# Four heads interleaved per group of cells, with K and V transposed four heads at a time, in an attention backward kernel

## Chip, cores and metric

One core of one Trainium2 chip. The metric is the time of one execution on the device, in microseconds (us); lower is better.

## The reference

Two independent blocks A and B of multi-head attention, each over 8 batches (b) of 96 queries with 32 heads (h) of 128 dimensions and a cache of 512 keys and values; forward output and all gradients, in bf16.

```python
def ref(x, k_cache, v_cache, wq, wo):        # x 8x96x640, caches 8x32x512x128
    q = (x @ wq).reshape(B, Sq, H, Dh).transpose(0, 2, 1, 3)
    p = softmax(einsum("bhqd,bhkd->bhqk", q, k_cache) * Dh ** -0.5)
    o = einsum("bhqk,bhkd->bhqd", p, v_cache)
    return o.transpose(0, 2, 1, 3).reshape(B, Sq, H * Dh) @ wo
# result: concat of blocks A and B, and its vjp with grad_out:
# dx, dk_cache, dv_cache, dwq, dwo of both blocks
```

Of the traffic, K and V are read twice each (once transposed), and dK and dV are written once: 256 KB per pair of heads and batch for each of them.

## The kernel before: what the change and the argument touch

The work is cut into 512 cells, one for each block, head and batch. A cell passes through stages in successive ticks. Two heads interleave, so 16 ticks carry two heads over 8 batches. The head work (projections, transposes of weights, gradients of the weights) is laid between the cells by a table of ticks.

```python
OFF = dict(t=-1, kn=3, vn=0, s2=3, s3=3, s4=4, s5=5, s6=6, s7=7, s8=8)   # tick offsets
HP = 2                                     # heads that interleave
TB = 2                                     # batches whose transposes are issued together

def p_ldT(h, b, which):                    # transposing DMA, K or V of HP heads
    t_ = kvp.tile([128, F4 * KC, 16], BF16, name=key + "_p", bufs=(4 if which == 0 else 6))
    src = (kc if which == 0 else vc)[b, h:h + HP].rearrange("h (r f) d -> (h r) (f d)", r=R8)
    nc.sync.dma_start_transpose(t_[:], src)                 # R8 = 16 // HP

def p_ldn(h, b, which):                    # plain load of the same K or V
    t_ = kvp.tile([128, HP, KC, 128], BF16, name=key, bufs=4)
    nc.sync.dma_start(...)

def p_st(h, b, which):                     # store of dV (1) or dK (0) of two heads
    nc.sync.dma_start(dst.rearrange("h (p c) d -> p h (c d)", c=KC), t_[:])

def c_s7(h, b):                            # dK, then evacuated by ACT
    ...
    st["dK_p"] = wk.tile([128, HP, KC * 128], BF16, name="dK_sb", bufs=2)
    nc.scalar.activation(dK_p[:, j], dK_ps[:], ACT.Identity, scale=1.0)
```

Note that every DMA above is issued by SP, one after the other: transposes, plain loads and stores (of the 1538 issues on SP in the trace of this kernel, no two overlap). dK_sb has two buffers, each for two heads.

## Time and profile before

| | |
|---|---|
| time, median of 2 runs | 1772.82 us (1771.46 to 1774.17) |
| span of the profiled run | 1763.2 us |
| PE content (instruction counts times their undisturbed durations) | 1591 us |
| transposing DMAs | 512 of 256 KB, 16 packets of 16 KB each |
| time for which SP is held by one of them | 1.75 us in the mean, 896 us in all |

The page and the waits are shown in the prediction below. What matters later and is not there is SP's own timeline. This is a stretch of it from the trace of the kernel before, with ACT's two evacuations of dK for one pair of heads (columns: start, duration, engine, line, operation, and in brackets the idle time before it):

```profile
641.02 0.60 ACT L428 ACTIVATE dK_sb<-dK_ps 128x512 bf16<-128x512 f32 x1
645.14 0.59 ACT L428 ACTIVATE dK_sb<-dK_ps 128x512 bf16<-128x512 f32 x1
```

```profile
645.22 3.01 SPq L246 DMA_TRANSPOSE KT_p<-in_A_k_cache_dram  x1
648.33 0.54 SPq L257 DMA_DIRECT2D V_sb<-in_A_v_cache_dram  x1
648.95 0.42 SPq L266 DMA_DIRECT2D out_dram<-dK_sb  x1
```

The pair of dK is complete at 645.73 us. Its store is issued at 648.95, 3.2 us later, after a transpose of K that held SP for 3.01 us and a plain load. What stands behind the transpose in SP's queue isn't issued in that time. Here the store still landed before ACT needed its buffer.

### The profile page before, as it was taken

Reading aid. Unit: us, or ns where it says so; the run is one execution under the profiler, and the core shown is the slowest. Engines: PE = TensorE matmul, PEld = TensorE weight load, DVE = VectorE, ACT = ScalarE, POOL = GpSimd, SP = SyncE. Lnnn points to the kernel's source line nnn. Section 1 sums busy time; section 2 is a strip of 40 time slices with the busy share of each in tenths; the row PEclk is TensorE's granted clock in tenths of the full one; section 3 lists DMA queues with packets and bytes.
Section 4 is the critical chain, followed back from the end, with each engine's and each line's share of the span. In section 5 each row is a group of like instructions: output and inputs, shape, how many; then the busy total and the mean of one; then the engine's idle time right before and its main releaser. Section 6 shows DMA issues by size and latency. Waiting matters only on the chain. (4 is left out here: it accounts for less than half of the span.)

```text
span 1763.2 us, 59487 instructions
## 1 busy us (share of the span) xinstructions
PE 1643.4 (93%) x22474; PEld 1371.8 (78%) x22648; DVE 1392.3 (79%) x3597; ACT 1349.2 (77%) x3529; POOL 712.9 (40%) x1306
## 2 busy tenths in 40 slices
PE   5899989999999999998998999999999989999997
PEld 4787878788888888786886787877878878787776
DVE  4786868878888888887886778787888878888885
ACT  4888967878778787875876898786787867878782
POOL 3343434433433443434365344343443334343336
PEclk9899999999999999999999999999999999999999
DMA  9999999999999999999999999999999999999983
GB/s 267 262 280 258 265 251 262 270 261 273 266 266 284 264 268 257 273 271 259 242 278 282 262 268 273 249 268 252 264 265 269 262 239 265 267 269 246 263 249 111
DMA packets 320609, 458.39 MB, mean 260 GB/s; under 512 B 37216, under 2 KB 300896, under 8 KB 312128
## 3 DMA queue, kind: packets, MB, share of 16 engines
q1 hardware_dynamic: 304672, 404.75, 87.7%
q0 software_dynamic: 15648, 49.83, 8.4%
q8 instruction: 177, 2.90, 0.7%
q14 instruction: 112, 0.92, 0.1%
HBM read 161.09 MB, written 159.12 MB: 182 GB/s over the span
## 5 line engine op out<-in xcount | busy, mean ns | idle before, releaser
L298 ACT ACTIVATE E_sb<-S_ps,negm 96x512 bf16<-96x512 f32 x512 | 349.2, 682 | 212.6 <-DVE negm L288 203.6
L317 POOL TENSOR_SCALAR P_sb<-E_sb,rinv 96x512 bf16<-96x512 bf16 x512 | 354.2, 692 | 343.8 <-DVE rinv L308 339.4
L371 POOL TENSOR_TENSOR prod<-OT_h,dOT_h 128x96 bf16<-128x96 bf16 x512 | 188.1, 367 | 571.6 <-DVE OT_h L343 563.0
L385 DVE SCALAR_TENSOR_TENSOR dS_sb<-dP_ps,dl_ps,P_sb 96x512 bf16<-96x512 f32 x512 | 382.1, 746 | 35.4 <-PE dl_ps L383 22.4
L288 DVE TENSOR_REDUCE negm<-S_ps 96x1 f32<-96x512 f32 x512 | 347.9, 680 | 67.4 <-PE S_ps L286 66.6
L428 ACT ACTIVATE dK_sb<-dK_ps 128x512 bf16<-128x512 f32 x512 | 302.6, 591 | 108.9 <-PE dK_ps L423 70.4
L362 ACT ACTIVATE dV_sb<-dV_ps 128x512 bf16<-128x512 f32 x512 | 307.8, 601 | 26.0 <-DMA out_dram<-dV_sb 23.3
L346 ACT ACTIVATE PT_sb<-optp_ps 128x384 bf16<-128x384 bf16 x512 | 252.1, 492 | 0.9 <-PE optp_ps L340 0.5
L286 PE MATMUL S_ps<-KT_p,QT_h 128*96 128x512 bf16 x512 | 197.1, 385 | 18.6 <-ACT dK_sb L428 18.1
L357 PE MATMUL dV_ps<-dOnat_h,P_sb 96*128 96x128 bf16 x2048 | 200.4, 221 | 6.1 <-ACT dV_sb L362 6.1
L423 PE MATMUL dK_ps<-Qnat_h,dS_sb 96*128 96x128 bf16 x2048 | 199.9, 221 | 6.1 <-ACT dV_sb L362 5.8
L407 PE MATMUL dq_dst_ps<-ident,dS_sb 96*128 96x96 bf16 x2048 | 174.4, 208 | 27.9 <-DVE dS_sb L385 26.0
L381 PE MATMUL dP_ps<-VT_p,dOT_h 128*96 128x512 bf16 x512 | 197.3, 385 | 0.9 <-ACT dV_sb L362 0.9
L409 DVE COPY dST_sb<-dq_dst_ps 128x384 bf16<-128x384 bf16 x512 | 177.5, 347 | 15.3 <-PE dq_dst_ps L407 14.5
L333 PE MATMUL optp_ps<-PT_sb,V_sb 128*128 128x96 bf16 x2048 | 173.5, 207 | 5.2 <-ACT PT_sb L346 5.1
L340 PE MATMUL optp_ps<-ident,P_sb 96*128 96x96 bf16 x2048 | 173.4, 206 | 2.6 <-POOL P_sb L317 2.0
L400 PE MATMUL dq_dst_ps<-dST_sb,K_sb 128*128 128x96 bf16 x2048 | 172.9, 208 | 2.7 <-ACT dK_sb L428 2.5
L510 PE MATMUL o_ps<-wo_r,OT_h 128*128 128x256 bf16 (+1 forms) x1152 | 154.7, 259 | 1.4 <-ACT E_sb L298 0.3
L400 PEld LDWEIGHTS <-K_sb 128*128 128x128 bf16 x2048 | 135.9, 99 | 23.2 <-issue 3.6
L343 DVE CAST OT_h<-optp_ps 128x96 bf16<-128x96 f32 x512 | 126.8, 248 | 34.1 <-PE optp_ps L340 31.0
L510 PE MATMUL o_ps<-wqT_h,dQT_h 128*128 128x256 bf16 (+1 forms) x1152 | 150.4, 255 | 0.0
L308 DVE RECIPROCAL rinv<-rowsum 96x1 f32<-96x1 f32 x512 | 79.9, 156 | 87.5 <-ACT E_sb L298 65.8
(77 smaller groups left out, 3398.3 us busy)
## 6 DMA issues: line engine op xcount, KB each, us to landing
out_dram<-dV_sb SPq DMA_DIRECT2D x256, 256.0 KB, 4.1
out_dram<-dK_sb SPq DMA_DIRECT2D x256, 256.0 KB, 4.0
V_sb<-in_A_v_cache_dram SPq DMA_DIRECT2D x128, 256.0 KB, 4.0
K_sb<-in_A_k_cache_dram SPq DMA_DIRECT2D x128, 256.0 KB, 4.4
V_sb<-in_B_v_cache_dram SPq DMA_DIRECT2D x128, 256.0 KB, 4.0
K_sb<-in_B_k_cache_dram SPq DMA_DIRECT2D x128, 256.0 KB, 4.8
out_dram<-dwo_sb POOLq DMA_DIRECT2D x64, 160.0 KB, 5.0
out_dram<-dwq_sb POOLq DMA_DIRECT2D x32, 320.0 KB, 6.0
```

The source lines that it names most:

```text
L288: nc.vector.tensor_reduce(negm[:], S_ps[:], axis=AX.X, op=ALU.max, negate=True)
L298: nc.scalar.activation(E_sb[:].rearrange("q (a f) -> q a f", f=F4), st["S_ps"][:].rearrange("q (f a) -> q a f", f=F4), ACT.Exp, bias=st["n ...
L317: nc.gpsimd.tensor_scalar(P_sb[:], st["E_sb"][:], st["rinv"][:], 0.0, op0=ALU.mult, op1=ALU.add)
L346: nc.scalar.activation(PT_sb[:], PT_ps, ACT.Identity, scale=1.0)
L357: nc.tensor.matmul(dV_ps[:, c * 128:(c + 1) * 128], P_sb[:, c * 128:(c + 1) * 128], hs["dOnat_h"][:, b * 128:(b + 1) * 128], start=True, s ...
L362: nc.scalar.activation(dV_p[:, j], dV_ps[:], ACT.Identity, scale=1.0)
L381: nc.tensor.matmul(dP_ps[:], hs["dOT_h"][:, tok], st["VT"], start=True, stop=True)
L385: nc.vector.scalar_tensor_tensor(dS_sb[:].rearrange("q (a f) -> q a f", f=F4), dP_ps[:].rearrange("q (f a) -> q a f", f=F4), dl_ps[:, 0:1] ...
L400: nc.tensor.matmul(dQT_ps, st["K_sb"][:, c, :], st["dST_sb"][:, c * Sq:(c + 1) * Sq], start=(c == 0), stop=(c == KC - 1))
L423: nc.tensor.matmul(dK_ps[:, c * 128:(c + 1) * 128], dS_sb[:, c * 128:(c + 1) * 128], hs["Qnat_h"][:, b * 128:(b + 1) * 128], start=True, s ...
L428: nc.scalar.activation(dK_p[:, j], dK_ps[:], ACT.Identity, scale=1.0)
L510: nc.tensor.matmul(o_ps[:], src[:, t * 128:(t + 1) * 128], rhs, start=(hh == 0), stop=(hh == groups[g] - 1))
```

## The change

Intent: fewer and larger transposing DMAs (half the count, 16 rows of 32 KB instead of 16 KB), and head work that is spread more evenly, as four heads now share 32 ticks. SBUF pays for it: several buffers become shallower.

```diff
-OFF = dict(t=-1, kn=3, vn=0, ...)
-HP = 2
-TB = 2
+OFF = dict(kt=-1, vt=2, kn=4, vn=1, ...)
+HP = 4          # heads that interleave, and heads of one transposing DMA
+NP = 2          # heads of one plain load or store
 HK = [          # ticks of the head work
-    dict(pA=-10, pB=-7, ...), dict(pA=-4, pB=-2, ...)
+    dict(pA=-14, pB=-10, ...), dict(pA=-12, pB=-6, ...), dict(pA=-8, pB=-1, ...),
+    dict(pA=-6, pB=0, pC0=[2, 3], pC1=[3, 4], pD1=5, pD0=7),
 ]
+GU0 = (9, 7)    # output work of a group: first tick, number of ticks
@@ loads of block B's x and gradient: still two per tick, 8 ticks earlier, but into one buffer
-            stp=P(name="stp", bufs=3),
+            stp=P(name="stp", bufs=1),
@@ buffers
-  wq_p [128, DC, 2 * 128] bufs=2          KT_p bufs=4, VT_p bufs=6 (two heads)
+  wq_p [128, DC, 4 * 128] bufs=1          KT_p bufs=2, VT_p bufs=2 (four heads)
-  K_sb, V_sb bufs=4    P_sb 5    PT_sb, dS_sb, dST_sb 3    dwo_sb 2    ob 5
+  K_sb, V_sb bufs=3    P_sb 4    PT_sb, dS_sb, dST_sb 2    dwo_sb 1    ob 3
-  QT_h, dOT_h bufs=4    Qnat_h, dOnat_h 3
+  QT_h, dOT_h bufs=6    Qnat_h, dOnat_h 5
@@ issue of loads and stores, per batch b and head j of the group
+                    em.add(ct + OFF["kt"], SLOTS["LOAD"], p_ldT(h, b, 0))   # j == 0
+                    em.add(ct + OFF["vt"], SLOTS["LOAD"], p_ldT(h, b, 1))   # j == 0
+                if j % NP == 0:
                     em.add(ct + OFF["kn"], SLOTS["LOAD"], p_ldn(h, b, 0))
                     em.add(ct + OFF["vn"], SLOTS["LOAD"], p_ldn(h, b, 1))
-                    em.add(ct + HP + OFF["s4"], SLOTS["LOAD"], p_st(h, b, 1))
-                    em.add(ct + HP + OFF["s7"] + 1, SLOTS["LOAD"], p_st(h, b, 0))
+                    em.add(ct + NP + OFF["s4"], SLOTS["LOAD"], p_st(h, b, 1))
+                    em.add(ct + NP + OFF["s7"] + 1, SLOTS["LOAD"], p_st(h, b, 0))
```

More of the change, by code (lines that the diff above doesn't have):

```diff
@@ L42 @@
 SL_SETUP = 96
-OFF = dict(t=-1, kn=3, vn=0, s2=3, s3=3, s4=4, s5=5, s6=6, s7=7, s8=8)
-HP = 2
-TB = 2
+OFF = dict(kt=-1, vt=2, kn=4, vn=1, s2=3, s3=3, s4=4, s5=5, s6=6, s7=7, s8=8)
+HP = 4
+NP = 2
 HK = [
-    dict(pA=-10, pB=-7, pC0=[-6, -4], pC1=[-5, -3], pD1=-2, pD0=0, qA0=21, qA1=25, qB=[28, 25], qD=[(26, 0, 2), (27, 2, 5)]),
-    dict(pA=-4, pB=-2, pC0=[-1, 3], pC1=[1, 2], pD1=3, pD0=6, qA0=29, qA1=33, qB=[36, 33], qD=[(34, 0, 2), (35, 2, 5)]),
-]
+    dict(pA=-14, pB=-10, pC1=[-9, -8], pC0=[-7, -6], pD1=-5, pD0=-4),
+    dict(pA=-12, pB=-6, pC1=[-5, -4], pC0=[-3, -2], pD1=1, pD0=4),
+    dict(pA=-8, pB=-1, pC0=[0, 1], pC1=[2, 3], pD1=4, pD0=6),
+    dict(pA=-6, pB=0, pC0=[2, 3], pC1=[3, 4], pD1=5, pD0=7),
+]
+for _j in range(4):
+    _t = 32 + 8 + 6 * _j
+    HK[_j].update(qA0=_t, qB=[_t + 1, _t + 2], qA1=_t + 3, qD=[(_t + 4, 0, 2), (_t + 5, 2, 5)])
+GU0 = (9, 7)
+GU1 = (16, 6)
 EV = dict(pB0="act", pB1="dve", pC00="act", pC01="act", pC10="act", pC11="dve", pD0="dve", pD1="dve", qA0="dve", qA1="dve", qB0="act", qB1="act", qD="dve", gU="act")
-GSPREAD0 = 9
 PRIO_OFF = 2000
-GSPREAD1 = 9
 SLOTS = dict(LOAD=0, S2A=5, S2B=5.5, S8=10, S7=20, S5=30, S4=40, S6=50, S3A=52, S3B=53, S5B=54, HEAD=SL_HEAD, GRP=SL_GRP)
@@ L150, in build_block @@
         if not first:
-            em.add(tick0 - 12 + c - 2, SL_LOAD, setup_ld(0, c))
-            em.add(tick0 - 11 + c - 2, SL_LOAD, setup_ld(1, c))
-        em.add(tick0 - 12 + c, SL_SETUP, setup_T(0, c))
-        em.add(tick0 - 11 + c, SL_SETUP, setup_T(1, c))
-    em.add(tick0 + (-15 if first else 21), SL_LOAD, setup_nat(1))
-    em.add(tick0 + (-16 if first else 20), SL_LOAD, setup_nat(0))
+            em.add(tick0 - 20 + c - 2, SL_LOAD, setup_ld(0, c))
+            em.add(tick0 - 19 + c - 2, SL_LOAD, setup_ld(1, c))
+        em.add(tick0 - 20 + c, SL_SETUP, setup_T(0, c))
+        em.add(tick0 - 19 + c, SL_SETUP, setup_T(1, c))
+    em.add(tick0 + (-25 if first else 30), SL_LOAD, setup_nat(1))
+    em.add(tick0 + (-26 if first else 33), SL_LOAD, setup_nat(0))
     def evac(eng, dst, src, sc=None):
@@ L175, in f @@
             if j == 0:
-                wq_p = hd.tile([128, DC, HP * 128], BF16, name="wq_p", bufs=2)
+                wq_p = hd.tile([128, DC, HP * 128], BF16, name="wq_p", bufs=1)
                 with nc.allow_non_contiguous_dma(reason="per-pair wq slice"):
@@ L198, in f @@
             st["wqT_h"] = wqT_h
-            st["QT_h"] = hd.tile([128, T], BF16, name="QT_h", bufs=4)
-            st["dOT_h"] = hd.tile([128, T], BF16, name="dOT_h", bufs=4)
+            st["QT_h"] = hd.tile([128, T], BF16, name="QT_h", bufs=6)
+            st["dOT_h"] = hd.tile([128, T], BF16, name="dOT_h", bufs=6)
         return f
@@ L226, in f @@
             src = st["QT_h"] if which == 0 else st["dOT_h"]
-            dst = hd.tile([Sq, B * 128], BF16, name="Qnat_h" if which == 0 else "dOnat_h", bufs=3)
+            dst = hd.tile([Sq, B * 128], BF16, name="Qnat_h" if which == 0 else "dOnat_h", bufs=5)
             st["Qnat_h" if which == 0 else "dOnat_h"] = dst
@@ L243, in f @@
             key = "KT" if which == 0 else "VT"
-            t_ = kvp.tile([128, F4 * KC, 16], BF16, name=key + "_p", bufs=(4 if which == 0 else 6))
+            t_ = kvp.tile([128, F4 * KC, 16], BF16, name=key + "_p", bufs=2)
             src = (kc if which == 0 else vc)[b, h:h + HP].rearrange("h (r f) d -> (h r) (f d)", r=R8)
@@ L254, in f @@
             key = "K_sb" if which == 0 else "V_sb"
-            t_ = kvp.tile([128, HP, KC, 128], BF16, name=key, bufs=4)
-            src = (kc if which == 0 else vc)[b, h:h + HP]
+            t_ = kvp.tile([128, NP, KC, 128], BF16, name=key, bufs=3)
+            src = (kc if which == 0 else vc)[b, h:h + NP]
             nc.sync.dma_start(t_[:].rearrange("p h c d -> p h (c d)"), src.rearrange("h (p c) d -> p h (c d)", c=KC))
-            for j in range(HP):
+            for j in range(NP):
                 CS[(blk, h + j, b)][key] = t_[:, j]
@@ L264, in f, with h_alloc @@
             t_ = CS[(blk, h, b)]["dV_p" if which == 1 else "dK_p"]
-            dst = (dv if which == 1 else dk)[b, h:h + HP]
+            dst = (dv if which == 1 else dk)[b, h:h + NP]
             nc.sync.dma_start(dst.rearrange("h (p c) d -> p h (c d)", c=KC), t_[:])
             if which == 0:
-                for j in range(HP):
+                for j in range(NP):
                     CS.pop((blk, h + j, b))
         return f
-    def h_alloc(h):
+    def h_alloc(h, name):
         def f():
-            st = HS[(blk, h)]
-            st["OT_h"] = hst.tile([128, T], BF16, name="OT_h", bufs=6)
-            st["dQT_h"] = hst.tile([128, T], BF16, name="dQT_h")
+            HS[(blk, h)][name] = hst.tile([128, T], BF16, name=name)
         return f
@@ L315, in f @@
                 st = CS[(blk, h, b)]
-                P_sb = wk.tile([Sq, Sk], BF16, name="P_sb", bufs=5)
+                P_sb = wk.tile([Sq, Sk], BF16, name="P_sb", bufs=4)
                 nc.gpsimd.tensor_scalar(P_sb[:], st["E_sb"][:], st["rinv"][:], 0.0, op0=ALU.mult, op1=ALU.add)
@@ L344, in f @@
             if k4 is not None:
-                PT_sb = wk.tile([128, KC * Sq], BF16, name="PT_sb", bufs=3)
+                PT_sb = wk.tile([128, KC * Sq], BF16, name="PT_sb", bufs=2)
                 nc.scalar.activation(PT_sb[:], PT_ps, ACT.Identity, scale=1.0)
@@ L357, in f @@
                 nc.tensor.matmul(dV_ps[:, c * 128:(c + 1) * 128], P_sb[:, c * 128:(c + 1) * 128], hs["dOnat_h"][:, b * 128:(b + 1) * 128], start=True, stop=True)
-            j = h % HP
+            j = h % NP
             if j == 0:
-                st["dV_p"] = wk.tile([128, HP, KC * 128], BF16, name="dV_sb", bufs=2)
+                st["dV_p"] = wk.tile([128, NP, KC * 128], BF16, name="dV_sb", bufs=2)
             dV_p = CS[(blk, h - j, b)]["dV_p"]
@@ L383, in f @@
             nc.tensor.matmul(dl_ps[:], st["prod"][:], ones[:, 0:1], start=True, stop=True)
-            dS_sb = wk.tile([Sq, Sk], BF16, name="dS_sb", bufs=3)
+            dS_sb = wk.tile([Sq, Sk], BF16, name="dS_sb", bufs=2)
             nc.vector.scalar_tensor_tensor(dS_sb[:].rearrange("q (a f) -> q a f", f=F4), dP_ps[:].rearrange("q (f a) -> q a f", f=F4), dl_ps[:, 0:1],
@@ L407, in f @@
                     nc.tensor.transpose(dST_ps[:, c * Sq:(c + 1) * Sq], dS_sb[:, c * 128:(c + 1) * 128], ident[0:Sq, 0:Sq])
-                dST_sb = wk.tile([128, KC * Sq], BF16, name="dST_sb", bufs=3)
+                dST_sb = wk.tile([128, KC * Sq], BF16, name="dST_sb", bufs=2)
                 nc.vector.tensor_copy(dST_sb[:], dST_ps)
@@ L423, in f @@
                 nc.tensor.matmul(dK_ps[:, c * 128:(c + 1) * 128], dS_sb[:, c * 128:(c + 1) * 128], hs["Qnat_h"][:, b * 128:(b + 1) * 128], start=True, stop=True)
-            j = h % HP
+            j = h % NP
             if j == 0:
-                st["dK_p"] = wk.tile([128, HP, KC * 128], BF16, name="dK_sb", bufs=2)
+                st["dK_p"] = wk.tile([128, NP, KC * 128], BF16, name="dK_sb", bufs=2)
             dK_p = CS[(blk, h - j, b)]["dK_p"]
@@ L449, in f @@
             if "dwo_sb" not in st:
-                st["dwo_sb"] = hd.tile([128, D], BF16, name="dwo_sb")
+                st["dwo_sb"] = hd.tile([128, D], BF16, name="dwo_sb", bufs=1)
                 st["dwo_n"] = 0
@@ L466, in f @@
             dQnat = st["dQnat"]
-            j = h % HP
+            j = h % NP
             pr = HS[(blk, h - j)]
             if "dwq_sb" not in pr:
-                pr["dwq_sb"] = hd.tile([128, DC, HP * 128], BF16, name="dwq_sb", bufs=1)
+                pr["dwq_sb"] = hd.tile([128, DC, NP * 128], BF16, name="dwq_sb", bufs=1)
                 pr["dwq_n"] = 0
@@ L481, in f @@
             pr["dwq_n"] += ncn
-            if pr["dwq_n"] == DC * HP:
+            if pr["dwq_n"] == DC * NP:
                 with nc.allow_non_contiguous_dma(reason="per-pair dwq slice"):
-                    nc.gpsimd.dma_start(dwq_v[:, :, (h - j) * 128:(h - j + HP) * 128], dwq_sb[:])
+                    nc.gpsimd.dma_start(dwq_v[:, :, (h - j) * 128:(h - j + NP) * 128], dwq_sb[:])
         return f
@@ L511, in f @@
             if NG == 1:
-                ob = wk.tile([128, w], BF16, name="ob", bufs=5)
+                ob = wk.tile([128, w], BF16, name="ob", bufs=3)
                 evac(EV["gU"], ob[:], o_ps[:])
@@ L519, in f @@
             else:
-                ob = wk.tile([128, w], BF16, name="ob", bufs=5)
+                ob = wk.tile([128, w], BF16, name="ob", bufs=3)
                 nc.vector.tensor_tensor(ob[:], o_ps[:], acc[:, t, c0:c0 + w], op=ALU.add)
@@ L536, in build_block @@
             em.add(c0t + hk["pB"], SL_HEAD, pB(h))
-            em.add(c0t + OFF["s5"], SL_LOAD, h_alloc(h))
+            em.add(c0t + j + OFF["s5"], SL_LOAD, h_alloc(h, "OT_h"))
+            em.add(c0t + j + OFF["s8"], SL_LOAD, h_alloc(h, "dQT_h"))
             for si in range(NTS):
@@ L545, in build_block @@
                 if j == 0:
-                    if b % TB == 0:
-                        for which in (0, 1):
-                            for bb in range(b, b + TB):
-                                em.add(ct + OFF["t"], SLOTS["LOAD"] - 1, p_ldT(h, bb, which))
+                    em.add(ct + OFF["kt"], SLOTS["LOAD"], p_ldT(h, b, 0))
+                    em.add(ct + OFF["vt"], SLOTS["LOAD"], p_ldT(h, b, 1))
+                if j % NP == 0:
                     em.add(ct + OFF["kn"], SLOTS["LOAD"], p_ldn(h, b, 0))
                     em.add(ct + OFF["vn"], SLOTS["LOAD"], p_ldn(h, b, 1))
-                    em.add(ct + HP + OFF["s4"], SLOTS["LOAD"], p_st(h, b, 1))
-                    em.add(ct + HP + OFF["s7"] + 1, SLOTS["LOAD"], p_st(h, b, 0))
+                    em.add(ct + NP + OFF["s4"], SLOTS["LOAD"], p_st(h, b, 1))
+                    em.add(ct + NP + OFF["s7"] + 1, SLOTS["LOAD"], p_st(h, b, 0))
                 em.add(ct + OFF["s2"], SLOTS["S2A"], c_s2a(h, b))
@@ L574, in build_block @@
         cLg = tick0 + (h0 + groups[g]) * B - 1
-        gs0 = max(3, (GSPREAD0 * groups[g]) // HG)
-        gs1 = max(3, (GSPREAD1 * groups[g]) // HG)
         em.add(cLg + OFF["s5"] - 2, SL_LOAD, gW(g))
-        subs = [(0, t, gi) for t in range(TT) for gi in range(len(gsplits))] + [(1, t, gi) for t in range(TT) for gi in range(len(gsplits))]
-        n_out = TT * len(gsplits)
-        for i, (which, t, gi) in enumerate(subs):
-            if which == 0:
-                tk = cLg + OFF["s5"] + 2 + (i * gs0) // n_out
-            else:
-                tk = cLg + OFF["s8"] + 2 + gs0 - 3 + ((i - n_out) * gs1) // n_out
-            em.add(tk, SL_GRP, gU(g, which, t, gi))
+        subs = [(t, gi) for t in range(TT) for gi in range(len(gsplits))]
+        for which, (g0, gn) in ((0, GU0), (1, GU1)):
+            for i, (t, gi) in enumerate(subs):
+                em.add(cLg + 1 + g0 + (i * gn) // len(subs), SL_GRP, gU(g, which, t, gi))
     pools["c_s45"] = c_s45
@@ L591, in _kernel_impl @@
 def _kernel_impl(tc, A_x, A_k_cache, A_v_cache, A_wq, A_wo, B_x, B_k_cache, B_v_cache, B_wq, B_wo, grad_out,
-           out_0, out_1, out_2, out_3, out_4, out_5, out_6, out_7, out_8, out_9, out_10, HG=4, slots=None, off=None, hk=None, ev=None, gspread=None, groupsA=None, groupsB=None):
-    global GSPREAD0, GSPREAD1
+           out_0, out_1, out_2, out_3, out_4, out_5, out_6, out_7, out_8, out_9, out_10, HG=4, slots=None, off=None, hk=None, ev=None, groupsA=None, groupsB=None):
     nc = tc.nc
@@ L602, in _kernel_impl @@
         EV.update(ev)
-    if gspread:
-        GSPREAD0, GSPREAD1 = gspread
     with ExitStack() as ctx:
@@ L626, in _kernel_impl @@
         em = Emitter()
-        t_next = 20
+        t_next = 28
         for blk, args in enumerate(((A_x, A_k_cache, A_v_cache, A_wq, A_wo, grad_out, out_0, out_1, out_2, out_3, out_4, out_5),
```

## The prediction

> **What bounds the kernel now.** I read the page's engine line first, then the slices, the DMA queues, the waits, one window of the chain, and the DMA issues around the change from block A to block B.
>
> ```profile
> PE 1643.4 (93%) x22474; PEld 1371.8 (78%) x22648; DVE 1392.3 (79%) x3597; ACT 1349.2 (77%) x3529; POOL 712.9 (40%) x1306
> ...
> DMA  9999999999999999999999999999999999999983
> ...
> q1 hardware_dynamic: 304672, 404.75, 87.7%
> q0 software_dynamic: 15648, 49.83, 8.4%
> ```
>
> Two resources look full: PE (93% of 1763.2 us) and the DMA engines (nines in every slice; 87.7 + 8.4 + 0.8% of 16 engines' span). Which one sets the pace? The waits decide:
>
> ```profile
> ACT dK_sb L428 <- DMA out_dram<-dK_sb: 24.5, 20, 3.3
> ...
> ACT dV_sb L362 <- DMA out_dram<-dV_sb: 23.3, 16, 3.3
> ...
> PE dq_dst_ps L407 <- DVE dS_sb L385: 26.0, 26, 1.6
> PE S_ps L286 <- ACT dK_sb L428: 18.1, 13, 3.3
> PE tp_ps L131 <- DMA ld_tmp<-in_B_x_dram: 6.3, 3, 4.0
> ```
>
> No matmul of the steady state waits for K, V or their transposes. The DMA reaches PE only through late stores: ACT may not overwrite dK_sb or dV_sb (48 us in 36 waits), and PE then waits for ACT (18 us at S_ps). One such chain, word for word:
>
> ```profile
> 1096.63 5.87 DMA out_dram<-dK_sb
> ...
> 1102.59 0.61 ACT dK_sb L428
> ...
> 1103.24 0.38 PE S_ps L286
> 1103.62 0.22 PE o_ps L510 x2
> 1103.83 0.17 PE dq_dst_ps L400 x4
> ```
>
> PE is otherwise dense: four 96-column matmuls follow each other in 0.17 us. From start to start, the median matmul takes 43, 56, 109 and 217 ns at 96, 128, 256 and 512 columns. The instruction counts times these give a **PE content** of 1591 us (some 512-column records are missing in the trace, so I count instructions, not records). The span is therefore 1591 content + 30 lost to a half clock (sum over the clock records) + some 142 of idle PE. Of that, by subtraction, about 17 lies before the first cell ends, 11 after the last, the rest between cells.
>
> I cut the span at each dl_ps matmul into 511 cells ("ticks") and compared each tick's length with its content. In the undisturbed groups of four heads (32 ticks, some 104.5 us) PE idles 5.3 us. Ticks with over 3.4 us of content lose almost nothing; those with under 2.6 us lose most, since a tick without head work holds only 1.6 us for PE while ACT and DVE have over 2 us each. So the kernel is PE-bound where head work lies and bound by ACT, DVE or a store where it doesn't.
>
> **What the Trainium skill says.**
> - "Perfetto Trace Analysis", Identifying the Most-Contended Engine: matmul busy share is a bad measure because matmuls are pipelined, and occupancy of 16 DMA engines misleads. The trace agrees: 97% DMA occupancy, yet no steady wait for a load.
> - "DMA: Bandwidth & Descriptors", Why a DMA increments its semaphore by 16 and not by 1: the engines of one DMA finish independently. For transposes the trace differs. Each of the 512 is 16 packets of 16 KB, one per engine; those packets start up to 2 us apart but end within some 20 ns. Lone ones take 726 ns, the mean is 1329: engines that started early wait for the last.
> - Same page, Anatomy of one DMA: about 2.0 us + bytes / 436e3. For a 192 KB ld_tmp that is an estimate of 2.5 us; this trace has 4.0 to 6.8, and I use the trace.
> - "TensorE: Matmul & The Clock Gate", What's actually happening: an idle window of about 3.4 us halves PE's clock. The trace has half-clock stretches of 3.4 or 6.8 us, one at 1104.4 us just after the stall above, though that stall was only 2.1 us.
>
> **The change part by part.**
>
> *Transposes.* 512 DMAs of 256 KB become 256 of 512 KB; bytes stay. Waste today is (1329 - 740) ns x 8192 packets / 16 engines = 301 us of engine span, with 740 taken for an unhindered packet. With the same loss per DMA at half the count, 150 us of occupancy go, and its share falls from 97% to about 89%. On PE's path only late stores count: some 30 us of PE waiting behind ACT (18 at S_ps, 6 + 6 at dV_ps and dK_ps) plus some 17 us of half clock after such stalls (six stretches in mid-run). I expect half of these 47 to go: **-24 us**. Half, because the dK and dV buffers stay at two and a store may now queue behind a 32 KB row, twice as long.
>
> *Head work.* The instruction order of both builds has the same PE instructions. Per group: 99 us of PE content in both; per tick the standard deviation falls from 0.71 to 0.59 us. With DVE and ACT content scaled to their busy union (0.88 and 0.82 of the sum of durations), the excess of the largest engine over PE in windows of two and three ticks falls from 4.8 and 2.9 us to 2.9 and 1.4 per group. Part of the first figure is elastic, so I take 1 us per group: 16 x 1 = **-16 us**.
>
> *Shallower buffers that stay harmless.* K_sb and V_sb fall from 4 to 3 pairs, transposes to two buffers of four heads. Counting ticks from release to next use, a load keeps four ticks (some 13 us) against 5 us to land. P_sb, PT_sb, dS_sb, dST_sb keep one spare tick.
>
> *ld_tmp, 3 buffers to 1.* Block B's x and gradient come in 10 chunk loads, transposed on PE at two per tick. In the new order, nine loads wait for the transposes of the chunk before them, and PE, in order, waits for the load:
>
> ```profile
> DMA to landing us min/median/max: 4.0/6.0/6.8
> ```
>
> Nine rounds of about 5 us = 45 us, of which the five ticks' ordinary work covers some 17: 28 us of stall, less the 6 us it costs now, plus 3 for half clock: **+25 us**.
>
> *ob, 5 buffers to 3.* The last group of each block writes 36 ob tiles, each stored before its buffer is reused. Issues near the block change, then near the end:
>
> ```profile
> out_dram<-ob POOLq DMA_DIRECT2D x24, 64.0 KB, 5.1
> ...
> out_dram<-ob POOLq DMA_DIRECT2D x24, 64.0 KB, 1.8
> ```
>
> Mid-run a buffer's round is 0.4 (DVE) + 5.1 + handovers, near 5.5 us; 12 rounds of three tiles = 66 us, but they are spread on 13 ticks = 43 us, and with DVE stalled stores land sooner: I take **+18 us**. In the tail a round is about 3 us, 36 us in all against 25 now: **+10 us**.
>
> *Lead-in and tail.* Head work moves out of mid-run: PE content before the first cell 15 to 24 us, after the last 22 to 30. It's the same work, so no cost by itself; the unfilled transposes-copy-matmul hops of the last heads and the 320 KB store at the end cost some **+3 us**.
>
> Sum: -24 - 16 + 25 + 18 + 10 + 3 = +16 us, say +10 as these stalls hide some bubbles: 1772.8 + 10 = about 1783 us.
>
> **Rivals.**
> 1. *The DMA engines are the true bound.* For it: occupancy, and SP busy issuing most of the time. Against it: no PE wait for a load, and ticks rich in head work run at content. If so, 150 us of freed occupancy would show as 40 to 60 us even after the one-off stalls: 1715 to 1735.
> 2. *Larger transposes hurt the stores.* A 512 KB transpose holds all 16 rings for about 1.5 us plus skew, on SP's in-order queue. Store landing of 4.0 us would rise and the 48 us of ACT waits grow to perhaps 80: near 1820.
> 3. *The one-off stalls are small*, since PE and POOL run ahead and stalls empty the DMA queues (4.0 us landings, overlapping work): the evening out wins, 1740 to 1755.
>
> **Range and chances.** The gains are 40 +/- 20 and the losses 56 +/- 20, both from few events; combined some +/- 28, so 1742 to 1815 for 8 in 10. Under 1737 (faster by 2%) needs rival 1, or the full 47 with rival 3: 0.08. Over 1808 needs rival 2 or the stalls at full size: 0.17. The rest, 0.75, is same.
>
> **What would show it.** Transposes: 256 issues, DMA share of q1 near 80%, waits of ACT on dK and dV stores under 30 us. Head work: a steady group of 32 ticks near 102 us, against 104.5. ld_tmp: a PE wait of some 28 us at tp_ps. ob: DVE waits on ob stores of over 25 us against 13.2 now, and a longer tail. I'm wrong if ld_tmp and ob waits stay under 20 us together, if S_ps or dP_ps come to wait for KT or VT, or if store waits grow.

## More of the kernel before

How such a duration is to be read: the Trainium skill ("Perfetto Trace Analysis", Per-instruction lifecycle) says that the recorded time of a DMA on its issuing engine begins when its semaphores are satisfied and ends when all its descriptors (the orders to the DMA engines) have been generated and the issuing engine is free for its next instruction.

## The result, and the profile after

The changed kernel took **1891.61 us** in the median of 2 runs (1884.56 to 1898.65), against 1772.82. Ratios here are the mean time of one kernel's fast runs over that of the other's fast runs of the same rounds, so they are not quite the ratio of the quoted medians. The ratio is 1.067, 95% interval 1.0496 to 1.0845: slower, and above the predicted range.

The share of time for which the DMA queue of the loads and stores was busy fell to what was predicted (87.7% before):

```profile
q1 hardware_dynamic: 292384, 404.72, 79.2%
```

The waits of the changed kernel (engine, tile and line, what ended the wait: total us, times, longest us):

```profile
ACT dK_sb L431 <- DMA out_dram<-dK_sb: 78.3, 44, 5.5
...
PE dwo_ps L459 <- ACT dK_sb L431: 33.5, 15, 4.0
...
DVE ob L524 <- DMA out_dram<-ob: 23.4, 16, 3.1
PE q_ps L224 <- ACT woT_h L165: 22.3, 17, 1.4
...
PE tp_ps L136 <- DMA ld_tmp<-in_B_x_dram: 14.3, 4, 4.1
```

That is a smaller saving than it looks, as the span had grown: the queue's busy time fell from 1546 to 1491 us, by 55 us and not by the predicted 150. ACT's waits for dK stores tripled, from 24.5 us; those for dV stores fell from 23.3 to 3.1. PE inherits ACT's waits at whatever comes next in its order of instructions, here most often dwo_ps. New is a wait on woT_h, the transposed output weights.

What a late dK store looks like in the trace of the changed kernel, first ACT and PE:

```profile
688.83 0.60 ACT L431 ACTIVATE dK_sb<-dK_ps 128x512 bf16<-128x512 f32 x1
...
701.25 0.60 ACT L431 ACTIVATE dK_sb<-dK_ps 128x512 bf16<-128x512 f32 x1 [3.65 <-DMA out_dram<-dK_sb]
```

```profile
701.90 0.59 PE L459 MATMUL dwo_ps<-g_nat,Onat 128*128 128x512 bf16 x1 [4.03 <-ACT dK_sb L431]
```

then SP over the same time:

```profile
687.76 4.68 SPq L251 DMA_TRANSPOSE VT_p<-in_A_v_cache_dram  x1
692.54 0.53 SPq L271 DMA_DIRECT2D out_dram<-dV_sb  x1
693.16 3.55 SPq L251 DMA_TRANSPOSE KT_p<-in_A_k_cache_dram  x1
696.83 0.51 SPq L262 DMA_DIRECT2D V_sb<-in_A_v_cache_dram  x1
697.44 0.41 SPq L271 DMA_DIRECT2D out_dram<-dK_sb  x1
```

and the stretch of 5 us in which PE resumes, from the table of windows (busy us and instruction counts of each engine, PE's granted clock, DMA share, GB/s):

```profile
700.14:705.14 5.00, 3.02 (x9) 1.37 (x10) 0.16 (x1) 2.74 (x7) 0.69 (x1) 0.51 1.23 346
```

The pair of dK is complete at 689.43 us. Its store is issued 8.0 us later, because SP is busy with the issue of a V transpose for 4.68 us and of a K transpose for 3.55 us. From the end of the issue to ACT's restart only 3.4 us pass. So the store is late in SP's queue, not in the DMA engines. PE stands still for 4.03 us and then runs at half clock (0.51).

I did this for every dK store in both traces (time from the end of the second evacuation to the start of the issue on SP, then from the end of the issue to the start of the ACT instruction that waited; "late" are the stores for which ACT waited):

| | before | changed |
|---|---|---|
| SP held by one transpose, mean | 1.75 us (512) | 3.44 us (256) |
| dK stores over 5 us in the queue, of 256 | 30 | 53 |
| the late ones: complete to issue | 4.4 us | 5.9 us |
| of which in the issue of transposes | 3.1 us | 4.3 us |
| of which in waits for buffers ahead of any issue | 0.4 us | 0.4 us |
| the late ones: end of the issue to ACT's restart | 4.7 us | 3.7 us |

The total hold on SP is the same (896 and 882 us), but it comes in pieces of twice the length, and a piece that falls ahead of a dK store is not made good by another that doesn't.

The changed kernel's trace holds a control of its own. In SP's order, 125 dK stores have two transposes between themselves and the dK store before, and 129 have none. The first kind stands in the queue for 4.55 us in the mean, and all 53 stores over 5 us are among them; the second kind stands there for 0.99 us. From issue to landing the first kind is the quicker one (median 3.8 us against 4.8).

Why does a larger transpose hold SP for longer? I matched each to its 16 packets (they end together, so they can be grouped by their ends) and compared the time at which SP was free again with the start of the packets:

| medians | 256 KB, before | 512 KB, changed |
|---|---|---|
| SP free, relative to the start of the first packet | 0.87 us before it | 1.57 us after it |
| SP free, relative to the start of the last of the 16 packets | 1.58 us before it | 0.26 us after it |
| share in which SP is free before the first packet starts | 99% | 1% |
| correlation of SP's hold with the time to the last packet's start | 0.49 | 0.97 |

A 256 KB transpose is handed over as a whole and SP goes on. With a 512 KB transpose SP is free only after the last of the 16 packets has begun, in 94% of the cases. That the engines' backlog sets this time is argued from the correlation and not shown. A part of the hold comes with the size alone: of the transposes whose last packet began within 2.1 us of the start of the issue, those of 512 KB still held SP for 2.46 us in the median (27 cases), those of 256 KB for 1.10 us (30 cases). The skill's diagram in that same section shows engines that start before the hand-over ends because a descriptor buffer is full; that a full buffer is the reason here fits the numbers but no run shows it.

The span, cut at the dl_ps matmuls as in the prediction ("excess" is a stretch's length less its PE content):

| us | before | changed | difference |
|---|---|---|---|
| excess before the first cell | 17.0 | 19.5 | +2.5 |
| excess around the block change (2 of 16 groups of 32 ticks) | 27.5 | 74.3 | +46.8 |
| excess of the other 14 groups | 116.4 | 175.9 | +59.5 |
| excess after the last cell | 10.9 | 21.5 | +10.6 |

Half-clock losses (30 us before, 51 after) are inside these rows; 17 of the 21 us that they grew by lie in the row of the block change. Over the 11 undisturbed groups, the median excess of each tick sums to 6.1 us before and 10.9 after; after the change, 4.1 us of it lie at tick 3, where the dK waits fall, right behind the four ticks in which PE's content is light (31, 0, 1 and 2, some 2 us each), and 1.6 at tick 29, the wait on woT_h.

### The profile page after: what moved, and what is told of

Same layout as the page of the kernel before. It is cut to its first block, busy times and chain, and to the rows that moved or that the text cites.

```text
span 1882.8 us, 59436 instructions
## 1 busy us (share of the span) xinstructions
PE 1693.1 (90%) x22505; PEld 1374.8 (73%) x22648; DVE 1402.0 (74%) x3597; ACT 1353.6 (72%) x3529; POOL 696.6 (37%) x1290
## 3 DMA queue, kind: packets, MB, share of 16 engines
q1 hardware_dynamic: 292384, 404.72, 79.2%
## 4 chain that ended last, share of the span: by engine, by line
PE 32%; DVE 6%; DMA 6%; ACT 4%; issue 3%; POOL 2%; POOLq 0%; ACTq 0%; DVEq 0%; SPq 0%
PE q_ps L224 5%; DMA out_dram<-dK_sb 4%; PE o_ps L513 4%; PE dwo_ps L459 3%; PE dwq_ps L481 3%; PE S_ps L289 3%; DVE negm L291 2%; PE dP_ps L384 2%; PE dK_ps L426 2%; PE dV_ps L360 2%; ACT E_sb L301 2%; PE dq_dst_ps L410 2%; PE optp_ps L343 2%; PE dq_dst_ps L403 2%; PE optp_ps L336 2%
## 5 line engine op out<-in xcount | busy, mean ns | idle before, releaser
L289 PE MATMUL S_ps<-KT_p,QT_h 128*96 128x512 bf16 x512 | 204.1, 399 | 8.0 <-ACT dK_sb L431 5.1
L384 PE MATMUL dP_ps<-VT_p,dOT_h 128*96 128x512 bf16 x512 | 204.2, 399 | 3.3 <-DVE ob L524 3.3
L410 PE MATMUL dq_dst_ps<-ident,dS_sb 96*128 96x96 bf16 x2048 | 174.8, 208 | 27.9 <-DVE dS_sb L388 24.5
L459 PE MATMUL dwo_ps<-g_nat,Onat 128*128 128x128 bf16 (+1 forms) x718 | 140.4, 311 | 41.9 <-ACT dK_sb L431 33.5
L403 PEld LDWEIGHTS <-K_sb 128*128 128x128 bf16 x2048 | 132.7, 99 | 23.3 <-issue 2.9
L513 PE MATMUL o_ps<-wo_r,OT_h 128*128 128x256 bf16 (+1 forms) x1152 | 148.2, 264 | 0.2 <-ACT E_sb L301 0.2
```

The lines of the kernel that those rows point to most:

```text
L289: nc.tensor.matmul(S_ps[:], hs["QT_h"][:, tok], st["KT"], start=True, stop=True)
L384: nc.tensor.matmul(dP_ps[:], hs["dOT_h"][:, tok], st["VT"], start=True, stop=True)
L403: nc.tensor.matmul(dQT_ps, st["K_sb"][:, c, :], st["dST_sb"][:, c * Sq:(c + 1) * Sq], start=(c == 0), stop=(c == KC - 1))
```

## The experiments

All times below are medians of 4 runs, beside 7 runs of the kernel before in the same rounds and on the same chip (the first batch ran on another chip than the two later ones). "Before" was 1764.3 us in the first batch (the first four runs), 1765.0 in the second, 1760.4 in the third. All results were correct. Ratios are against before, with their 95% intervals; the changed kernel itself, at 1.067, was timed in two runs only, so small differences from it are not resolved. Against a threshold of 2%, runs 1, 2 and 7 are slower, runs 10 and 12 the same; in all the others the difference from before is clear of noise, but on which side of 2% it lies is unclear.

### 1. Transposes of two heads again

The changed kernel with one part undone.

```diff
-R8 = 16 // HP ... name=key + "_p", bufs=2 ... [b, h:h + HP]     # issued for j == 0
+R8 = 16 // NP ... name=key + "_p", bufs=4 ... [b, h:h + NP]     # issued for j % NP == 0
```

> The changed kernel with one part undone: each transposing DMA again loads two heads as 16 rows of 16 KB (512 issues, four buffers of two heads, the same memory); the order of cells, head work and all other buffers stay as changed. Theory A (the large transposes hold the 16 rings and SP's in-order queue, so dK stores land late): ACT's waits for dK and dV stores fall from 81 us to 48 us or less, the PE idle of 4 us in tick 3 of each group of 32 shrinks below 1.5 us, and the time falls by 50 us or more, to 1820 to 1845. Theory B (four ticks without head work in a row make the cells ask for more bytes per time than the DMA engines give, whatever the size of the transposes; the wq_p load falls in the same place): the store waits stay at 65 us or more and the time within 25 us of 1892, or gets worse, since twice as many transposes each wait for their slowest engine.

Measured: 1817.8 us, ratio 1.031 (1.027 to 1.035). Waits of this run:

```profile
ACT dK_sb L431 <- DMA out_dram<-dK_sb: 24.3, 21, 2.2
PE q_ps L224 <- ACT woT_h L165: 22.3, 17, 1.4
```

The headline part of the change costs by itself some 65 us (1.067 less 1.031; 33 to 94 us over the changed kernel's interval). The dK waits return to those of before, and tick 3 falls from 4.1 us to about 1. The other 53 us come from the rest of the change.

### 2. Output work of a group moved into the light ticks

```diff
-GU0 = (9, 7)
+GU0 = (6, 10)
```

> The changed kernel with one schedule constant changed: the output projection of a group starts at tick 6 of the next group and is spread over 10 ticks instead of starting at 9 over 7, so that the four ticks with only 1.9 to 2.0 us of PE content get 0.7 to 0.9 us each. Theory B (light ticks in a row outrun the DMA): the 4 us of PE idle in tick 3 of each group falls below 2 us, waits for stores fall below 60 us, and the time falls by 25 to 50 us. Theory A (large transposes): little change, under 15 us, since the transposes stay. In either case the ob waits near the change of block should fall a little, 24 ob tiles of 36 having more time.

Measured: 1863.5 us, ratio 1.0546 (1.0469 to 1.0623), inside the interval of the changed kernel, so the time alone is inconclusive. The dK waits rose to 93.6 us in 58 waits; the light ticks were filled and the stall at tick 3 went, but ticks 2 and 15 took up 1.8 and 1.1 us. So the light ticks decide where the stall is paid; as the dK waits did not fall with them, they are not what makes the stores late.

### 3. The kernel before with the shallower buffers

```diff
-  KT_p 4, VT_p 6, K_sb/V_sb 4, P_sb 5, PT_sb/dS_sb/dST_sb 3, dwo_sb 2
+  KT_p 4, VT_p 4, K_sb/V_sb 3, P_sb 4, PT_sb/dS_sb/dST_sb 2, dwo_sb 1
```

> The kernel before with the shallower working buffers of the change alone: K_sb and V_sb 3, VT 4 buffers of two heads, P_sb 4, PT_sb, dS_sb, dST_sb 2, dwo_sb 1; ob and ld_tmp as they were. My prediction called these harmless: within 10 us of 1773. Rival (the shallower buffers cost part of the steady loss of some 5 us per group): 1800 or more, with new PE waits at S_ps, dP_ps or the optp and dq_dst matmuls.

Measured: 1791.7 us, ratio 1.0164 (1.0123 to 1.0204). Waits:

```profile
ACT dK_sb L428 <- DMA out_dram<-dK_sb: 53.2, 40, 3.3
PE S_ps L286 <- ACT dK_sb L428: 24.0, 16, 3.8
```

The prediction called these buffers harmless. They cost 27 us, and again as dK stores that are late in SP's queue (41 of them over 5 us in it, against 30).

### 4. The kernel before with few buffers for one-off work

```diff
-  ob bufs=5, ld_tmp (pool stp) bufs=3
+  ob bufs=3, ld_tmp (pool stp) bufs=1
```

> The kernel before with only ob at 3 buffers instead of 5 and the chunk loads of block B's x and gradient at 1 instead of 3. My prediction put these one-off stalls at 25 (chunk loads) + 18 (ob at the block change) + 10 us (ob in the tail) in the changed kernel; here the ob writes are spread over 18 ticks instead of 13, so ob should cost less: 25 + 5 + 10 = 40 us, 1800 to 1825. If they are under 20 us, those terms of the prediction were too high and more of the loss belongs to the steady part.

Measured: 1801.7 us, ratio 1.0212 (1.0156 to 1.0267): 37 us. Waits:

```profile
DVE ob L521 <- DMA out_dram<-ob: 27.9, 19, 4.7
...
PE tp_ps L131 <- DMA ld_tmp<-in_B_x_dram: 13.8, 4, 3.6
```

The excess around the block change is 58.9 us against 27.5, and the tail is 8 us longer. The 37 us are near the 40 that the expectation of this run names.

### 5 and 6. The changed kernel with dK stores issued elsewhere

This tells a wait in SP's queue from a wait in the DMA engines. Bytes, data and buffers stay; only the issuing engine differs.

```diff
-nc.sync.dma_start(dst..., t_[:])
+(nc.gpsimd if which == 0 else nc.sync).dma_start(dst..., t_[:])     # run 5
+(nc.scalar if which == 0 else nc.sync).dma_start(dst..., t_[:])     # run 6
```

> The changed kernel, with the stores of dK issued from POOL's queue instead of SP's; everything else as changed. In the trace of the changed kernel the 48 dK stores that ACT later waited for left SP's queue 5.9 us after their data was ready, 3.0 us of that behind a K transpose and 1.35 us behind a V transpose, and landed 3.7 us after their issue; in the kernel before 22 such stores stood 4.4 us in the queue and landed in 4.7 us. Theory Q (SP's queue is in order, and a transpose of four heads blocks it longer at a time): ACT's waits for dK stores fall from 78 us to under 25, and the time falls by 40 to 70 us, to 1820 to 1850, about the kernel with transposes of two heads (1818). Rival D (the stores are late in the DMA engines, behind the 32 KB packets): the waits stay above 60 us and the time within 15 us of 1891. Side effect to expect either way: 256 issues of 0.54 us on POOL, 138 us beside its 697 busy, which may delay P and cost 5 to 20 us.

> The same as the run before, but the dK stores are issued from ACT's queue, which writes dK itself. Theory Q: ACT's waits for dK stores under 15 us, time 1815 to 1850; the issues cost ACT about 256 x 0.4 = 100 us, which ACT (72% busy) mostly takes from its idle time. Rival D: waits above 60 us, time 1880 or more. If both this and the run before fall by the same amount, it is the queue and not the engine that issues.

Measured: 1808.5 us from POOL, ratio 1.024 (1.0187 to 1.0293), and 1808.4 from ACT, ratio 1.0235 (1.0173 to 1.0298). The dK waits, with POOL, then with ACT:

```profile
ACT dK_sb L431 <- DMA out_dram<-dK_sb: 0.4, 1, 0.4
```

```profile
ACT dK_sb L431 <- DMA out_dram<-dK_sb: 3.2, 3, 1.3
```

From the views of dK_sb, the time from issue to landing of these stores, in the changed kernel, then from POOL, then from ACT:

```profile
DMA to landing us min/median/max: 2.1/4.2/7.7
```

```profile
DMA to landing us min/median/max: 2.5/4.9/9.5
```

```profile
DMA to landing us min/median/max: 2.1/4.5/8.4
```

Landing got no quicker. What fell is the time in the queue: from 2.73 us in the mean to 0.58 and 0.56, with no store over 5 us. The transposes still hold SP for 3.5 us each (SP is still free only after the last packet's start, 0.27 and 0.29 us in the median). So theory Q stands, rival D falls: the place of the dK stores in SP's queue cost the changed kernel some 77 us (1.067 less 1.0235; 46 to 108 us over the changed kernel's interval). Both times came out below the ranges that theory Q named. Not all of this is due to the size of the transposes: the same move gains some 13 us with transposes of two heads (run 1 against run 9). That two engines as different as POOL and ACT give the same time shows that it is SP's queue that matters, not who issues instead. An issue took 0.76 us on POOL and 0.39 on ACT in the mean; the difference did not show in the time.

### 7. The fourth head's weight transposes later

```diff
-    dict(pA=-6, pB=0, pC0=[2, 3], pC1=[3, 4], pD1=5, pD0=7),
+    dict(pA=-6, pB=3, pC0=[3, 4], pC1=[4, 5], pD1=6, pD0=7),
```

> The changed kernel, with the fourth head's weight transposes moved from tick 0 to tick 3, so that they stand in the same tick as the projection that reads them and not behind the third head's. Theory B (a light head schedule with single buffers leaves bubbles): the waits of PE for ACT's woT evacuation fall from 22 us to under 5, the excess of tick 29 of a group from 1.6 us to about 0, time lower by 12 to 25 us (1866 to 1880). Rival: the bubble only moves to the store waits or to another tick, and the time stays within 8 us.

Measured: 1875.9 us, ratio 1.0619 (1.056 to 1.0679). Waits:

```profile
ACT dK_sb L431 <- DMA out_dram<-dK_sb: 104.3, 54, 8.7
...
PE q_ps L224 <- ACT woT_h L165: 0.5, 1, 0.5
```

The woT wait is gone, and tick 29 with it. The dK waits grew by 26 us in exchange, and tick 3 by 1.1 us. The time lies in theory B's range, but it can't be told from that of the changed kernel. Part of the rival holds: while SP's queue sets the pace, mending another bubble mostly moves the wait.

### 8. The kernel before with dK stores from ACT

> The kernel before, with its dK stores issued from ACT's queue. Theory Q: its 24.5 us of waits for dK stores fall under 8 and the time falls by 15 to 30 us, to 1735 to 1750. Rival: the 100 us of issue on ACT (77% busy here) delay E and dV by as much as is gained: within 8 us of 1765 or slower, with idle time of PE on ACT's tiles in place of it.

Measured: **1736.6 us**, ratio 0.9829 (0.9777 to 0.9881), with the same edit as in run 6. The dK waits fell from 24.5 us to

```profile
ACT dK_sb L428 <- DMA out_dram<-dK_sb: 4.1, 5, 1.8
```

The same queue was costing the kernel before some 28 us.

### 9. Large against small transposes, with the stores out of the way

The edits of runs 1 and 6 together.

> The changed kernel with two parts undone at once: transposes of two heads again (16 rows of 16 KB, four buffers each) and dK stores on ACT's queue. It stands beside the run with transposes of four heads and dK stores on ACT's queue (1808.4). Theory Q (all that the large transposes cost was the place of the dK stores behind them, and DMA occupancy bounds nothing): the two agree within 12 us, 1797 to 1820, although the packets of the queue take 5 to 6% more of the engines' time here. Rival O (the saved occupancy is worth something once the stores are out of the way): this run is slower than 1808 by 20 us or more.

Measured: 1801.5 us, ratio 1.0236 (1.0199 to 1.0274), against 1.0235 in run 6. With the stores out of SP's queue, the size of the transposes is worth nothing either way; rival O falls. The four ratios together show that the cost needs both, large transposes and the stores behind them:

| ratio to before | dK stores on SP | dK stores on ACT |
|---|---|---|
| transposes of four heads | 1.067 (changed) | 1.0235 (run 6) |
| transposes of two heads | 1.031 (run 1) | 1.0236 (run 9) |

What the larger transposes free of the DMA engines' time is worth nothing in this kernel. It is little: the queue of SP's DMAs is busy for 70.2% of the span in run 6 and for 73.2% in run 9.

### 10. The changed kernel with everything mended

dK stores from ACT, the edit of run 7, and:

```diff
-GU0 = (9, 7)                       wq_p of four heads, bufs=1
+GU0 = (6, 10)                      wq_p of two heads, bufs=2
-block B's columns: two loads and two transposes per tick
+block B's columns: one load and one transpose per tick, from tick -28
```

> The changed kernel with transposes of four heads kept and everything mended that the runs so far pointed to: dK stores on ACT's queue, the fourth head's weight transposes in tick 3, wq loaded for two heads into two buffers, the second block's column loads spread to one per tick, the group's output work two ticks earlier. From 1808: 24 us for the waits on woT (1.6 us at tick 29, 15 groups), 15 to 20 us for the waits on ld_tmp, 5 to 10 us for POOL's waits on wq_p: 1755 to 1775. If the light ticks were themselves a cost (rival B), it goes lower still, under 1750; if the bubbles only move, it stays above 1790.

Measured: 1758.6 us, ratio 0.9988 (0.9947 to 1.0028): the same as before, at the lower end of what was expected. The undisturbed groups now have a median excess of 3.0 us, less than run 8's 4.5: here the even spread of head work shows at last. What keeps it behind run 8 lies in the one-off parts: 54 us of excess around the block change against 29, and 17 against 11 after the last cell. Its largest wait on stores is

```profile
DVE ob L525 <- DMA out_dram<-ob: 27.7, 20, 4.9
```

More than three ob buffers were not run here. The kernel of this run does build with four, so whether they would help is open.

### 11. Shallow buffers with dK stores from ACT

The edits of runs 3 and 6 on the kernel before.

> The kernel before with the shallower buffers of the changed one (this alone cost 1.6%, 1791.7 against 1764.3) and dK stores on ACT's queue. Theory Q (shallow buffers hurt only because SP then waits longer for a free buffer with a dK store behind it): all of the 28 us come back, 1730 to 1748, beside 1736.6 with the deep buffers. Rival S (the shallow working buffers P, PT, dS, dST stall the engines themselves): 1755 or more.

Measured: 1725.4 us, ratio 0.9828 (0.9773 to 0.9883), against 0.9829 for run 8 with the deep buffers. All of the 27 us of run 3 come back. So the buffers are harmless to the engines, and rival S falls. That the loss passes through the dK stores is shown; the reason given in the expectation (SP waits longer for a free buffer) is not: in run 3 the late stores spent 3.6 us of their 5.2 us in the queue behind issues of transposes and only some 0.4 us behind waits for buffers. Why more of those issues fall ahead of a dK store with shallower buffers stays open.

### 12. dV stores from ACT as well

> The kernel before with both the dK and the dV stores on ACT's queue; with dK alone there it took 1736.6 and ACT still waited 10.6 us for dV stores. Theory Q: 1722 to 1735, waits for dV stores under 4 us. Rival: another 100 us of issues on ACT, which writes E for the critical chain, cost more than the 10 us: 1740 or more.

Measured: 1757.3 us, ratio 0.9994 (0.9955 to 1.0033): the gain of run 8 is gone, as the rival said. Its reason, ACT's 256 further issues of some 0.4 us, is not shown. Two of PE's waits grew:

```profile
PE optp_ps L333 <- ACT PT_sb L346: 13.2, 11, 1.8
...
PE S_ps L286 <- ACT dK_sb L428: 7.3, 6, 2.6
```

The first of these was 3.5 us in run 8, and more than half of it falls into the first 92 us; the second did not appear. The second is for the most part not a matter of ACT's issues: 5 of its 6 waits follow a dK store that was issued 0.03 us after its data was complete and landed only 8.7 to 10.4 us later, against 4.5 in the median. So here the landing was late, and a late store is not always a late issue. As other waits fell, PE's gaps (over 60 ns) grew only from 83 to 88 us in all, and the half-clock losses by 4 us. What takes the rest of the gain back stays open.

## Why the prediction was wrong, step by step

**What bounds the kernel: right.** No load of the steady state bounds PE, the occupancy that larger transposes free is worth nothing (run 9), and the DMA reaches PE there only through late stores.

**Transposes, -24 us: wrong, and this is the step that failed.** It read the stores as late because the DMA engines are busy, so that freed occupancy would halve the waits. The queue's share of the time fell as said (79.2%), but partly by luck, since the span grew: its busy time fell by 55 us in place of 150. "The same loss per DMA at half the count" was wrong. A packet took 0.60 us longer than the quickest 5% before (1329 ns in the mean against 726) and 0.90 us longer after (2406 against 1510). dV waits fell by 20 us, and dK waits rose by 54, which is one of the signs of being wrong that the prediction names. What the change made longer for a dK store is the time in SP's queue: the late ones stood in it for 4.4 us in the kernel before and for 5.9 after, while their landing got quicker. The data to see the queue were in the trace of before. The prediction named "a store may now queue behind a 32 KB row", but as a discount on a gain, and on the way to memory. It did not see that a transpose of twice the size keeps SP itself for twice as long (3.44 us against 1.75), in nearly all cases until the last of the 16 packets has begun, and so stops the queue of the stores. In place of -24 us the term is a loss of some 65 us (run 1).

**Head work, -16 us: not seen in the changed kernel.** The evenness was gained and given back. An undisturbed group of 32 ticks took 110.5 us in the median, against 105.5 before and a forecast of 102. Measured with the stores out of the way, the undisturbed groups have 6.0 us of excess (run 6) against 4.5 in the kernel before (run 8), 1.6 of it the woT wait that the new table brought: the third and the fourth head share one woT_h buffer within a few ticks. Without that and with the other mends (run 10) it is 3.0. Like for like, that is a gain of 1.5 us per group over run 8, near the 1 us predicted; it needed mends that the change did not have. The prediction compared the sums of work per window and did not check the single buffers that the new order passes through.

**"Shallower buffers that stay harmless": wrong as put.** They cost 27 us alone (run 3) and nothing once the dK stores have left SP's queue (run 11). The step asked whether a load still arrives in time; it does. It didn't ask what becomes of the stores that share SP with the loads, the same error as in the first step.

**ld_tmp +25, ob +18 and +10, ends +3: right in sum, not in its parts.** The block change cost 37 us in run 6 (65 - 27.5) and 47 in the changed kernel, against 43 predicted; the tail cost 10.6, the lead-in 2.5. But the waits were smaller than forecast (14.3 us at tp_ps against some 28, 23.4 on ob stores against over 25), and half-clock losses made up for it: they grew by 17 us around the block change, where 3 were predicted.

**Rivals.** Rival 1 (DMA bound) found no support: the occupancy that came free was small, and run 9 shows that it is worth nothing. Rival 2 described what came: waits "grow to perhaps 80" (81 us for dK and dV together) and "SP's in-order queue". Its time of 1820 kept the gain of the head work, which did not come. Rival 3 fell with run 4.

Left open: runs 5 and 6 take the stores out of SP's queue and also off that queue's rings in the DMA engines. The landing times, which did not fall, speak for the first. A run with the order on SP alone changed was not made; in a build with the dK store's place in the program a tick earlier, many of these stores still stood behind the K transpose. Also open are the reasons in runs 3 and 12, as said, and what sets the size from which a transpose holds its issuing engine.

## What to carry to other kernels

In these traces the DMAs of one engine are issued one after the other, and a transpose of twice the size held the queue for twice as long (3.44 us against 1.75). So check whether a store that frees a buffer stands behind large loads. Before judging a change of DMA sizes, measure for each late transfer the time from "data complete" to "issued" apart from "issued" to "landed": a fix of the one does nothing for the other (runs 5 and 6 fixed the first, and the second did not fall). One stream of stores on an engine with some idle time can be worth more than a larger transfer (run 8 against the changed kernel); a second stream took that gain back (run 12).

## What the Trainium skill lacked or had wrong

- "DMA: Bandwidth & Descriptors", Issuing engines are not separate DMA queues: it says that initiating DMAs on several engines only saves sequencer time, "which is usually small relative to the DMA itself". Here that time was the cost. A 512 KB transpose held SP for 3.44 us in the mean, against 5.5 to 6.5 us from its issue to its landing, and moving 256 stores to another engine took the ratio from 1.067 to 1.0235.
- "Perfetto Trace Analysis", Per-instruction lifecycle: its account of the recorded time is right here. It lacks the size at which the hand-over of a DMA stops being independent of the engines' backlog: SP was free before the first packet for 99% of the 256 KB transposes and for 1% of the 512 KB ones.
- "Perfetto Trace Analysis", DMA Optimizations: "Larger DMA sizes saturate HBM bandwidth better." Its examples are transfers of a few KB; these were large before. Doubling the transposes from 256 to 512 KB cost some 65 us (run 1) and, with the stores elsewhere, was worth nothing (ratios 1.0235 and 1.0236). The same list's advice to give inputs and outputs different issuing engines was the better one for the dK stores: 28 us on the kernel before. How many issues a busy engine bears it does not say: 256 on ACT gained, 512 did not.
- "DMA: Bandwidth & Descriptors", Why a DMA increments its semaphore by 16 and not by 1: the independence of the engines does not hold for transposing DMAs in these traces. The 16 packets of one end within 0.16 us in nine of ten cases (the prediction's 20 ns was too narrow), though they start 0.6 us (256 KB) to 1.2 us (512 KB) apart in the median.
